# Joining the low three bits of float64 weight words on VectorE: one OR in place of scaling, shift and integer add

## The chip, the cores and the metric

The kernel runs on one core of a Trainium2 chip. The metric is the device time of one execution in microseconds (us), the median of three executions. PE is TensorE (PEld its weight load), DVE VectorE, ACT ScalarE, POOL GpSimd, SP SyncE.

## What is computed

The reference is an attention block followed by a feed-forward block with two weight matrices:

```python
out_d = sm_attn(q_d, k_d, v_d)                  # pooled by 4 along the sequence
out_up = np.repeat(out_d, factor, axis=2)
scores = np.where(mask, scale * q @ k.T, -1e9)  # |i - j| < 4
out_local = softmax(scores) @ v
x = (out_up + out_local) as [4608 tokens, 512]
h = x @ w_in                                    # 512 x 2048
g = np.where(h >= 1, h, np.where(h <= -1, 0.0, (h + 1) ** 2 / 4))
out = g @ w_out                                 # 2048 x 512
```

The two weight matrices are given as float64. The kernel reads them as pairs of 32-bit words and forms the float32 bits itself.

## The kernel before

**Work and stages.** There are 32 attention units (8 batches, 4 pairs of heads), 11 token chunks (one of 512, eight of 384, two of 512) and 16 blocks of the feed-forward width (`f`). In the first stage, to about 144 us, everything stands in a list written out by hand (`ORDER`, L92): units 0 to 7 of the attention, the loading and decoding of all 32 weight blocks (`i0` to `i15` of `w_in`, `o0` to `o15` of `w_out`), and the feed-forward of the first chunk. After it a scheduler weaves the other 24 units between the matmuls of the other chunks (to about 730 us), and the last two chunks are multiplied with fewer products (`strassen`) to the end. Each engine runs its instructions in the order given; semaphores make it wait for others.

**A weight block** comes as `raw` (128 partitions, 512 numbers, two words each). `convert` (L798) decodes it in six pieces, each with a place of its own in `ORDER` (`i4.c1`, `i4.c3` ...):

- piece 1 (L803, ACT): the exponent of the high words is rebased in place;
- piece 3 (L816, DVE): `m` becomes the high words shifted left by three;
- piece 2: the low words, as unsigned numbers, times 2^-29, which rounds to an integer from 0 to 8. On ACT (L812) for 24 blocks, on DVE (L810) for the 8 blocks of `ON_VECTOR` (`o1, o3 ... o15`);
- piece 4 (L819, DVE): integer addition of the two, in place; the trace calls it CUSTOM_DVE_ANT_0, the built program ISA;
- piece 5 (L822, ACT): `m` rounded into the high part `w[:, 0]` of the weight;
- piece 6 (L826, POOL): the rest, `m` minus the high part, into `w[:, 1]`.

PE's products need both parts: each product is high by high, low by high and high by low.

**The tiles** `m`, `u`, `gh` and `gl` rotate through ten buffers of 128x512 (`temp`, L795). `m` is taken from them in piece 3.

**The first chunk's feed-forward** for each `f`: 12 matmuls (L847) into one of two banks, the gate (`u1` DVE L869, `sq` ACT L872, `u2` DVE L875, `gh` ACT L881, `gl` POOL L884), then 12 matmuls (L902).

**The attention units 4 to 7** of this stage share one PSUM tile (two banks, `hi1`): scores (L311, L323) are written to it, DVE takes the maximum (`mxl`, L334) and subtracts it (`sl`, L353), the pooled scores (L377) take the same tile after that, and at the end of the unit DVE's `x` (L541) reads the outputs, upon which the next unit's L311 may write.

Of the kernel before, what the change touches and what calls it, by code (L numbers as in the profile page):

```python
# [11 lines left out]
I32 = mybir.dt.int32  # L12
U32 = mybir.dt.uint32
U8 = mybir.dt.uint8
AF = mybir.ActivationFunctionType
ALU = mybir.AluOpType
# [11 lines left out]
NFC = DFF // P  # L28
# [52 lines left out]


WARM = 10
ON_VECTOR = {("o", f) for f in range(1, NFC, 2)}

PIECES = (3, 4, 2, 1)

# [73 lines left out]
def attention_then_ffn(ctx: ExitStack, tc, qT, kT, vw, vp, vq, band, members, w_in, w_out, out):  # L161
    nc = tc.nc
# [625 lines left out]
    raw, weights = {}, {}  # L788
# [6 lines left out]
    def temp(name, kind=F32):  # L795
        return mpool.tile([P, 512], kind, name=name, tag="t512", bufs=10)

    def convert(name, f, piece):  # L798

        t = raw[name, f]  # L800
        if piece == 1:
            high = t.bitcast(F32)[:, :, 1]
            nc.scalar.activation(high, high, AF.Prelu, scale=2.0**-112, alpha=-(2.0**32))  # L803
        elif piece == 2:
            raw["low", name, f] = t[:, :, 0]
            if (name, f, "m") in raw and (name, f) not in ON_VECTOR:
                raw["low", name, f] = t.rearrange("p n t -> p (n t)")[:, 0:512]
            low = t.bitcast(U32)[:, :, 0]
            if (name, f) in ON_VECTOR:
                nc.vector.tensor_scalar(raw["low", name, f], low, 2.0**-29, None, op0=ALU.mult)  # L810
            else:
                nc.scalar.activation(raw["low", name, f], low, AF.Copy, scale=2.0**-29)  # L812
        elif piece == 3:
            raw[name, f, "m"] = temp("m")
            mi = raw[name, f, "m"].bitcast(I32)
            nc.vector.tensor_scalar(mi, t[:, :, 1], 3, None, op0=ALU.logical_shift_left)  # L816
        elif piece == 4:
            mi = raw[name, f, "m"].bitcast(I32)
            nc.vector.tensor_tensor(mi, mi, raw["low", name, f], op=ALU.add)  # L819
        elif piece == 5:  # L820
            w = wpool.tile([P, 2, 512], F32R, name=f"w_{name}{f}", tag=f"w{name}{f}")
            nc.scalar.copy(w[:, 0], raw[name, f, "m"])  # L822
            weights[name, f] = w
        else:
            w = weights[name, f]
            nc.gpsimd.tensor_tensor(w[:, 1], raw[name, f, "m"], w[:, 0], op=ALU.subtract)  # L826
# [233 lines left out]
    with psum("pair") as two, tc.manual_schedule(), ExitStack() as six:  # L1060
# [7 lines left out]
        for token in ORDER:  # L1068
            token, _, spare = token.partition("+")
            spare = int(spare or 0)  # L1070
            token, _, tag = token.partition("@")
            whose, what = token.split(".")
            kind, f = whose[0], whose[1:]
            if kind in "io":
                if what == "ld":
                    load_weights(kind, int(f))
                else:
                    convert(kind, int(f), int(what[1]))
            elif kind == "f":
                c, f = divmod(int(f), NFC)  # L1080
                if not banks:
                    six.close()
                    single(six, ["h0"], ["o0"], ["o1", "o2"], ["h1"], ["o3"])
                if what[1:].isdigit() and what[0] == "s":
                    keep_up(banks["o0"][:, 0:P], spare)
                    product(c, f, int(what[1]))
                else:
                    gate(c, f, what)
            elif kind == "m":
                second_product(0, int(f), int(what))  # L1090
            elif tag:
                ops[int(whose)][what](own[tag], tag, spare)
            elif spare:
                ops[int(whose)][what](spare)
            else:
                ops[int(whose)][what]()
# [162 lines left out]
```

## Time and profile before

| what | us |
|---|---|
| median of three executions | 897.67 |
| lowest and highest | 896.5, 898.2 |
| the profiled execution, first to last instruction | 900.0 |
| PE busy in it | 885.3 (98%) |
| DVE busy | 563.7 (63%) |
| ACT busy | 467.9 (52%) |
| POOL busy | 375.0 (42%) |

No other time of the profiled execution is given than its span, which stands 2.3 us (0.3%) above the median. Matmuls are pipelined and their ends are modelled, so a busy share of PE tells only where it was idle. In lists of groups the first number behind the bar is the time in which the group ran, the second the mean of one instruction in ns, the third the time the engine sat idle just before it and who ended that. In timelines a bracket holds the idle time before a row. DVE instructions that follow each other without a wait overlap by about 0.07 us, so their durations sum to a little more than their distance.

### The profile page before, as it was taken

The page shows a single profiled execution, that of the slowest core. Times are in us where ns is not written, and L with a number is a line of the kernel's source. Part 1 is how long each engine was busy: PE and PEld are TensorE (multiplying, and loading weights), DVE is VectorE, ACT ScalarE, POOL GpSimd, SP SyncE. Part 2 cuts the span into 40 slices and gives each one's busy share as a digit, 9 for nine tenths or more (in the row PEclk, how much of TensorE's full clock was granted, in tenths as well). Part 3 has the DMA queues.
Part 4 walks back from the last instruction along what each step waited for, and adds up shares of the span by engine and source line. Part 5 has one row for each costly group of instructions (what it writes and reads, how often), then busy time and mean ns, then how long its engine had stood idle before and what let it go on. Part 6 is the DMA issues. An engine that isn't in the chain of part 4 may idle for free.

```text
span 900.0 us, 19773 instructions
## 1 busy us (share of the span) xinstructions
PE 885.3 (98%) x7808; PEld 798.0 (89%) x7808; DVE 563.7 (63%) x1077; ACT 467.9 (52%) x1025; POOL 375.0 (42%) x361
## 2 busy tenths in 40 slices
PE   8999899999999999999999999999999999999998
PEld 6687688899999999999999999989999989999997
DVE  6699995766566477566556656665556546754442
ACT  4798675554544545554454454564454444434333
POOL 3166783444343244444432443344444434433232
PEclk9999999999999999999999999999999999999999
DMA  9369311333233233333332343342233212434341
GB/s 344 120 213 319 126 57 53 97 110 128 90 115 115 91 106 116 122 120 116 113 103 89 101 133 103 105 139 92 91 127 106 83 51 83 122 109 141 105 126 53
DMA packets 67884, 106.47 MB, mean 118 GB/s; under 512 B 5808, under 2 KB 33456, under 8 KB 67792
## 3 DMA queue, kind: packets, MB, share of 16 engines
q1 hardware_dynamic: 67648, 105.17, 35.5%
q8 instruction: 61, 1.00, 0.4%
q14 instruction: 31, 0.25, 0.1%
q10 hardware_dynamic: 144, 0.05, 0.0%
HBM read 71.51 MB, written 17.83 MB: 99 GB/s over the span
## 4 chain that ended last, share of the span: by engine, by line
PE 84%; DVE 7%; ACT 4%; issue 3%; POOL 2%; DMA 0%; SPq 0%; DVEq 0%; ACTq 0%; POOLq 0%
PE ffn_o L902 37%; PE ffn_h L847 28%; PE ffn_h L1015 7%; PE score_ps L643 2%; PE turn_ps L771 1%; PE value_ps L667 1%; DVE m L819 1%; PE local_ps L768 1%; PE value_ps L625 1%; DVE m L816 1%; DVE u L869 1%; DVE u L875 1%; POOL gl L884 1%; ACT u L872 1%; DVE sums L924 1%
## 5 line engine op out<-in xcount | busy, mean ns | idle before, releaser
L884 POOL TENSOR_TENSOR gl<-u,gh 128x384 fp32r<-128x384 f32 (+1 forms) x176 | 197.0, 1120 | 400.4 <-ACT gh L881 320.3
L902 PE MATMUL ffn_o<-w_o,gh 128*128 128x512 f32 x1152 | 347.5, 383 | 0.0
L847 PE MATMUL ffn_h<-xh,w_i 128*128 128x384 f32 (+1 forms) x1184 | 301.2, 336 | 2.5 <-POOL w_i L826 2.1
L902 PEld LDWEIGHTS ffn_o<-w_o,gh 128*128 128x128 f32 x1152 | 212.0, 190 | 25.2 <-issue 0.6
L847 PEld LDWEIGHTS ffn_h<-xh,w_i 128*128 128x128 f32 x1184 | 209.5, 189 | 16.9 <-POOL w_i L826 2.9
L902 PE MATMUL ffn_o<-w_o,gl 128*128 128x512 f32 x576 | 218.9, 380 | 0.4 <-POOL gl L884 0.4
L847 PE MATMUL ffn_h<-xl,w_i 128*128 128x384 f32 (+1 forms) x592 | 197.3, 333 | 0.0
L872 ACT ACTIVATE u<-u 128x384 f32<-128x384 f32 (+1 forms) x176 | 97.4, 553 | 133.5 <-DVE u L869 133.5
L881 ACT CAST gh<-u 128x384 fp32r<-128x384 f32 (+1 forms) x176 | 95.3, 542 | 118.8 <-DVE u L875 117.3
L869 DVE TENSOR_SCALAR u<-m 128x384 f32<-128x384 f32 (+1 forms) x160 | 76.1, 476 | 127.3 <-ACT m L868 126.9
L875 DVE SCALAR_TENSOR_TENSOR u<-m,u 128x384 f32<-128x384 f32 (+1 forms) x160 | 103.2, 645 | 78.0 <-ACT u L872 78.0
L902 PEld LDWEIGHTS ffn_o<-w_o,gl 128*128 128x128 f32 x576 | 109.3, 190 | 16.4 <-POOL gl L884 0.8
L847 PEld LDWEIGHTS ffn_h<-xl,w_i 128*128 128x128 f32 x592 | 111.9, 189 | 2.2
L868 ACT COPY m<-ffn_h 128x384 f32<-128x384 f32 (+1 forms) x132 | 63.8, 484 | 51.1 <-PE ffn_h L847 42.4
L720 ACT ACTIVATE sl<-sl 128x640 f32<-128x640 f32 x24 | 17.7, 739 | 55.1 <-POOL sl L694 55.1
L581 POOL TENSOR_TENSOR xl<-x,xh 128x576 fp32r<-128x576 f32 (+4 forms) x32 | 35.3, 1110 | 16.6 <-ACT xh L580 16.6
L826 POOL TENSOR_TENSOR w_o<-m,w_o 128x512 fp32r<-128x512 f32 x16 | 24.1, 1517 | 31.2 <-ACT w_o L822 31.2
L924 DVE SCALAR_TENSOR_TENSOR sums<-sums 128x128 f32<-128x128 f32 (+1 forms) x72 | 33.0, 459 | 1.6
L694 POOL TENSOR_TENSOR sl<-sl,mxl 128x640 f32<-128x640 f32 x24 | 30.2, 1260 | 2.3 <-DVE mxl L693 1.7
L924 DVE SCALAR_TENSOR_TENSOR words<-sums,words 128x512 fp32r<-128x512 f32 x16 | 17.7, 1109 | 17.7 <-ACT words L928 17.7
L826 POOL TENSOR_TENSOR w_i<-m,w_i 128x512 fp32r<-128x512 f32 x16 | 22.6, 1415 | 11.6 <-ACT w_i L822 11.4
L1041 POOL TENSOR_TENSOR m<-both 128x256 f32<-128x256 f32 x14 | 10.7, 765 | 39.0 <-DVE both L1040 33.8
(179 smaller groups left out, 1183.4 us busy)
## 6 DMA issues: line engine op xcount, KB each, us to landing
xh<-kept SPq DMA_DIRECT2D x56, 256.0 KB, 3.8
v<-vw SPq DMA_DIRECT2D x29, 320.0 KB, 4.0
vq_sb<-vq SPq DMA_DIRECT2D x24, 384.0 KB, 3.0
out<-osb SPq DMA_DIRECT2D x36, 256.0 KB, 2.4
raw_i<-w_in SPq DMA_DIRECT2D x16, 512.0 KB, 8.7
raw_o<-w_out SPq DMA_DIRECT2D x16, 512.0 KB, 8.9
kept<-words SPq DMA_DIRECT2D x32, 256.0 KB, 2.6
k_sb<-kT SPq DMA_DIRECT2D x28, 288.0 KB, 3.3
```

The costliest lines, as they stand in the source:

```text
L581: nc.gpsimd.tensor_tensor(xl[:, p, dst], x[:, part], xh[:, p, dst], op=ALU.subtract)
L826: nc.gpsimd.tensor_tensor(w[:, 1], raw[name, f, "m"], w[:, 0], op=ALU.subtract)
L847: ins = nc.tensor.matmul(htiles[c, f], wi[:, wt, cc * P : (cc + 1) * P], turns(xt[:, cc, ts]), start=(cc == 0 and xt is xh and wt == 0), s ...
L868: utiles["copied"] = nc.scalar.copy(m, h)
L869: nc.vector.tensor_scalar(utiles[c, f], m if c > 0 else h, -1.0, 1.0, op0=ALU.max, op1=ALU.add)
L872: nc.scalar.activation(u, u, AF.Square, scale=0.5)
L875: utiles["last"] = nc.vector.scalar_tensor_tensor(u, utiles["m"] if c > 0 else h, 1.0, u, op0=ALU.max, op1=ALU.min)
L881: nc.scalar.copy(gh, utiles[c, f])
L884: nc.gpsimd.tensor_tensor(gl, utiles.pop((c, f)), gh, op=ALU.subtract)
L902: ins = nc.tensor.matmul(o, gt[:, ts], turns(weights["o", f][:, wt, :]), start=f == 0 and n == 0, stop=f == NFC - 1 and n == 2,)
L924: return nc.vector.scalar_tensor_tensor(out, a, 1.0, b, op0=ALU.mult, op1=op)
L1015: ins = nc.tensor.matmul(ps, left(wt, k), right(xt, k), start=not more and k == 0 and wt == xt, stop=k == 1 and xt == 1, skip_group_check= ...
```

## The change

Pieces 2 and 3 do nothing any more. Piece 4 takes the tile `m` and issues two instructions on DVE: the low words times 2^-29, capped at 7, as integers into `m`; then the high words shifted left by three, OR `m`. The table `ON_VECTOR` goes. `ORDER` stays as it is, so both instructions stand where the addition stood.

```diff
@@ -81,7 +81,6 @@
 WARM = 10
-ON_VECTOR = {("o", f) for f in range(1, NFC, 2)}
@@ -801,22 +800,15 @@
         if piece == 1:
             high = t.bitcast(F32)[:, :, 1]
             nc.scalar.activation(high, high, AF.Prelu, scale=2.0**-112, alpha=-(2.0**32))
-        elif piece == 2:
-            raw["low", name, f] = t[:, :, 0]
-            if (name, f, "m") in raw and (name, f) not in ON_VECTOR:
-                raw["low", name, f] = t.rearrange("p n t -> p (n t)")[:, 0:512]
-            low = t.bitcast(U32)[:, :, 0]
-            if (name, f) in ON_VECTOR:
-                nc.vector.tensor_scalar(raw["low", name, f], low, 2.0**-29, None, op0=ALU.mult)
-            else:
-                nc.scalar.activation(raw["low", name, f], low, AF.Copy, scale=2.0**-29)
-        elif piece == 3:
+        elif piece in (2, 3):
+            return
+        elif piece == 4:
             raw[name, f, "m"] = temp("m")
             mi = raw[name, f, "m"].bitcast(I32)
-            nc.vector.tensor_scalar(mi, t[:, :, 1], 3, None, op0=ALU.logical_shift_left)
-        elif piece == 4:
-            mi = raw[name, f, "m"].bitcast(I32)
-            nc.vector.tensor_tensor(mi, mi, raw["low", name, f], op=ALU.add)
+            nc.vector.tensor_scalar(mi, t.bitcast(U32)[:, :, 0], 2.0**-29, 7.0, op0=ALU.mult, op1=ALU.min)
+            nc.vector.scalar_tensor_tensor(
+                mi, t[:, :, 1], 3, mi, op0=ALU.logical_shift_left, op1=ALU.bitwise_or
+            )
```

In the built program the lines below L84 stand one lower, those below piece 2 eight lower: the scaling is now L808, the join L809, `x` L540, `sl` L352.

DVE's order ahead of the `x` of unit 5, before (names end in buffer numbers; `raw_o10` is the block):

```order
L869 TENSOR_SCALAR u_1249<-ffn_h1_715 128x512
L816 TENSOR_SCALAR m_1264<-raw_o10_1145 128x512
L875 SCALAR_TENSOR_TENSOR u_1249<-ffn_h1_715,u_1249 128x512
L816 TENSOR_SCALAR m_1280<-raw_o9_1109 128x512
L816 TENSOR_SCALAR m_1287<-raw_i12_1213 128x512
L810 TENSOR_SCALAR raw_o9_1109<-raw_o9_1109 128x512
L819 ISA m_1264<-m_1264,raw_o10_1145 128x1024
L819 ISA m_1280<-raw_o9_1109,m_1280 128x1024
L816 TENSOR_SCALAR m_1332<-raw_i11_1167 128x512
L541 TENSOR_TENSOR x_1341<-pl_ps_1311,xd_1339 128x576
```

And with the change:

```order
L861 TENSOR_SCALAR u_1229<-ffn_h1_710 128x512
L867 SCALAR_TENSOR_TENSOR u_1229<-ffn_h1_710,u_1229 128x512
L808 TENSOR_SCALAR m_1274<-raw_o10_1128 128x512
L809 SCALAR_TENSOR_TENSOR m_1274<-raw_o10_1128,m_1274 128x512
L808 TENSOR_SCALAR m_1283<-raw_o9_1092 128x512
L809 SCALAR_TENSOR_TENSOR m_1283<-raw_o9_1092,m_1283 128x512
L540 TENSOR_TENSOR x_1314<-pl_ps_1286,xd_1312 128x576
```

Four weight instructions stand there in place of seven; the shifts of `i12` and `i11` went behind, to their additions.

DVE's order from the maximum of unit 6's scores (`mxl`) to its pooled sums, before:

```order
L816 TENSOR_SCALAR m_1400<-raw_o13_1236 128x512
L334 TENSOR_REDUCE mxl_1405<-sl_ps_1370 128x10
L810 TENSOR_SCALAR raw_o13_1236<-raw_o13_1236 128x512
L353 TENSOR_TENSOR sl_1418<-sl_ps_1370,mxl_1405 128x640
...
L291 TENSOR_REDUCE kd_1478<-k_sb_1428 128x144
L819 ISA m_1332<-m_1332,raw_i11_1167 128x1024
L819 ISA m_1287<-m_1287,raw_i12_1213 128x1024
```

And with the change:

```order
L333 TENSOR_REDUCE mxl_1375<-sl_ps_1342 128x10
L352 TENSOR_TENSOR sl_1387<-sl_ps_1342,mxl_1375 128x640
...
L290 TENSOR_REDUCE kd_1447<-k_sb_1397 128x144
L808 TENSOR_SCALAR m_1453<-raw_i11_1150 128x512
L809 SCALAR_TENSOR_TENSOR m_1453<-raw_i11_1150,m_1453 128x512
L808 TENSOR_SCALAR m_1460<-raw_i12_1187 128x512
L809 SCALAR_TENSOR_TENSOR m_1460<-raw_i12_1187,m_1460 128x512
```

Two instructions went from the path of `sl`, and two came in ahead of the weights `i11` and `i12`.

## Rows read from the trace of the kernel before

**Rows 1.** Stretches: length, busy us (instructions) by engine, PE clock, DMA share, GB/s.

```profile
60.00:80.00 20.00, 18.23 (x136) 14.91 (x133) 19.93 (x28) 18.09 (x34) 16.57 (x11) 1.00 0.82 269
80.00:100.00 20.00, 19.33 (x135) 15.97 (x133) 19.44 (x25) 17.70 (x30) 14.50 (x10) 1.00 0.50 196
...
120.00:140.00 20.00, 19.57 (x181) 16.07 (x180) 16.58 (x25) 12.89 (x22) 17.15 (x12) 1.00 0.21 66
140.00:160.00 20.00, 20.00 (x193) 17.40 (x192) 9.30 (x18) 10.59 (x23) 4.98 (x5) 1.00 0.21 72
```

**Rows 2.** What PE waited for, 0 to 145 us: total, times, longest.

```profile
PE sl_ps L311 <- DVE x L541: 2.3, 1, 2.3
PE ffn_h L847 <- POOL w_i L826: 2.1, 2, 1.8
PE sp_ps L377 <- DVE sl L353: 1.9, 2, 1.2
...
PE ffn_o L902 <- POOL gl L884: 0.4, 1, 0.4
```

**Rows 3.** PE's timeline, 75 to 110 us: start, length, line, shape, count, idle before.

```profile
75.52 0.48 PE L847 MATMUL ffn_h<-xh,w_i 128*128 128x512 f32 x1 [1.77 <-POOL w_i L826]
...
101.88 0.55 PE L311 MATMUL sl_ps<-band_r,ident_r 128*128 128x384 f32 x2 [2.26 <-DVE x L541]
...
103.21 1.22 PE L902 MATMUL ffn_o<-w_o,gh 128*128 128x512 f32 x2
...
109.13 0.71 PE L377 MATMUL sp_ps<-kd,first_qd 64*64 64x144 f32 x12 [0.75 <-DVE sl L353]
```

**Rows 4.** The stretch behind the longest stall, columns as in rows 1.

```profile
102.00:107.00 5.00, 5.00 (x52) 4.06 (x53) 5.00 (x7) 4.02 (x7) 2.09 (x3) 0.66 0.44 124
```

**Rows 5.** DVE's weight instructions L816, 57 to 101.9 us: busy us, count.

```profile
57.00:101.90 44.90, 12.40 (x16) 1.00 0.60 211
```

**Rows 6.** The same for L819.

```profile
57.00:101.90 44.90, 16.11 (x15) 1.00 0.60 211
```

**Rows 7.** The same for L810.

```profile
57.00:101.90 44.90, 2.61 (x3) 1.00 0.60 211
```

**Rows 8.** Three lines by themselves: count, then minimum, median, maximum in ns.

```profile
L810 DVE TENSOR_SCALAR raw_o<-raw_o x8: 418/534/1648, 33.9 to 131.7; 128x512 int32<-128x512 uint32 x8
...
L819 DVE CUSTOM_DVE_ANT_0 m<-m,raw_i x16: 669/693/1815, 31.7 to 133.8; 128x1024 uint16<-128x1024 uint16 x16
...
L826 POOL TENSOR_TENSOR w_i<-m,w_i x16: 1278/1294/1757, 40.3 to 135.9; 128x512 fp32r<-128x512 f32 x16
```

**Rows 9.** DVE by line and shape, whole span: two groups of SCALAR_TENSOR_TENSOR.

```profile
L924 DVE SCALAR_TENSOR_TENSOR words<-sums,words 128x512 fp32r<-128x512 f32 x16 | 17.7, 1109 | 17.7 <-ACT words L928 17.7
...
L875 DVE SCALAR_TENSOR_TENSOR u<-ffn_h,u 128x512 f32<-128x512 f32 x16 | 11.0, 690 | 1.0 <-ACT u L872 0.9
```

**Rows 10.** DVE's timeline ahead of `x` of unit 5 and ahead of `sl` of unit 6.

```profile
93.19 1.61 DVE L816 TENSOR_SCALAR m<-raw_i 128x512 int32<-128x512 int32 x1
94.72 1.56 DVE L810 TENSOR_SCALAR raw_o<-raw_o 128x512 int32<-128x512 uint32 x1
...
99.68 1.48 DVE L816 TENSOR_SCALAR m<-raw_i 128x512 int32<-128x512 int32 x1
101.08 0.74 DVE L541 TENSOR_TENSOR x<-pl_ps,xd 128x576 f32<-128x576 f32 x1
...
104.67 1.33 DVE L816 TENSOR_SCALAR m<-raw_o 128x512 int32<-128x512 int32 x1
...
106.65 1.65 DVE L810 TENSOR_SCALAR raw_o<-raw_o 128x512 int32<-128x512 uint32 x1
```

**Rows 11.** DVE's timeline, two instructions, the second on the first's output.

```profile
80.30 0.25 DVE L411 RECIPROCAL sp_ps<-sp_ps 128x13 f32<-128x13 f32 x1
80.59 0.82 DVE L415 TENSOR_TENSOR sl<-sl,sp_ps 128x640 f32<-128x640 f32 x1
```

**Rows 12.** ACT by line and shape, whole span: the scalings of piece 2.

```profile
L812 ACT ACTIVATE raw_i<-raw_i 128x512 int32<-128x512 uint32 x16 | 12.5, 797 | 0.0
```

## The prediction

> **What bounds the kernel now.** The profiled execution took 900.0 us from first to last instruction, 2.3 above the median of 897.67; the sums below are differences inside that execution, and I take them off the median unchanged. I read the stretches first [rows 1]: from 140 us on PE is busy all the time (20.00 of 20), so the change, whose 32 weight blocks are all decoded before that, can only move the first stage, and what it gains there the rest keeps. Between 60 and 100 us DVE is busy for 19.93 and 19.44 of 20 us, ACT for about 18, and PE is short of 20 by 1.8 and 0.7; between 120 and 140 DVE has 3.4 us to spare. Then PE's waits [rows 2]: 2.3 for DVE's `x`, 2.1 for the low part of an `i` block from POOL, 1.9 in two waits for DVE's `sl`, 0.4 for a `gl`: 6.7 us in all. In PE's timeline [rows 3] the long ones end at 75.52 (1.77 long), 101.88 (2.26) and 109.13 (0.75). After the 2.26 us a pair of matmuls of 512 columns takes 1.22 us; the stretch behind it [rows 4] was granted 0.66 of the clock, so that part of it ran at the lower level (1.2 GHz), and (1 - 0.66) x 5.0 = 1.7 us were lost by that. The wait of 1.77 us had no such fall behind it (the stretch from 60 to 80 has the clock at 1.00). Everything that can be won is thus 6.7 + 1.7 = 8.4 us, nearly 1%. A measurement of this kernel tells about 0.2% (1.8 us) from no change.
>
> **The change part by part.**
>
> *ACT.* 24 scalings of about 0.80 us [rows 12] go, 19 us. ACT is not named in front of PE's long waits; gates and the rounding of weights queue behind the scalings, though. I cost the relief at nothing in the sum, since DVE, full beside it, sets the pace; the bound above is the whole wait of 1.77, whose POOL instruction stands behind a `gl` that needs ACT.
>
> *DVE.* 32 shifts, 32 additions and 8 scalings (72 instructions) become 32 scalings and 32 joins (64). The new scaling is of the same kind as L810: unsigned words with a stride of two, multiplied, to integers; alone that takes 0.42 [rows 8], in the stretch 2.61 / 3 = 0.87 [rows 7]. I take 0.775, the mean of the 16 shifts there (12.40 / 16 [rows 5]), since both read one strided word stream and meet the same neighbours. The cap is a second operation in the same pass and I cost it at nothing. A join of integers isn't in the trace. Below I bound it by a free three-operand instruction, 0.69, above by one beside a busy POOL, 1.11 [rows 9]; I take 1.07, the mean of the 15 additions of the stretch (16.11 / 15 [rows 6]), which also read two tiles. New is a wait: the join needs its own scaling's result, at once. A dependent pair stands 0.04 us apart from end to start [rows 11], where free ones overlap by 0.07, so each pair pays about 0.12 more. A pair is then 0.775 + 1.07 + 0.12 = 1.97 us; its ends are 0.42 + 0.69 + 0.04 = 1.15 and 0.87 + 1.11 + 0.12 = 2.10. The tile `m` is taken at the scaling, later than the shift took it, so a buffer's last reader (a POOL low part, or PE's second product of an earlier `f`) has had longer to finish; queued behind such a wait would be everything on DVE, but the old shifts had the same kind of wait, and I cost it at nothing. The orders of PE, POOL and SP, loads included, stay as they were.
>
> The Trainium skill, "VectorE: DVE Perf Modes", section "The DRAIN you can't avoid", has it that a semaphore between two VectorE instructions costs nothing extra, since the pipe is emptied anyway. By that the 0.12 falls away, the 15 pairs before `x` would be 1.8 us shorter, and the sum below would come to about 5.9 in place of 4.1; the row, in which the waiting instruction starts later than a free one, decides against it.
>
> *The path to `x` of unit 5 (101.08 us), where PE waits longest.* DVE hardly idles from 57 us up to it, so what leaves the queue ahead of it counts in full. It had 16 shifts, 15 additions and 3 scalings there: 12.40 + 16.11 + 2.61 = 31.1 us [rows 5 to 7]. Now it has 15 pairs, 15 x 1.97 = 29.5: 1.6 saved. Counted at the place itself, three instructions go (a shift of 1.61, a scaling of 1.56 and a shift of 1.48 [rows 10], each less the overlap of 0.07): 4.4. The scaling of `o7` (median 0.53 [rows 8]) less its overlap adds 0.46; the waits take 15 x 0.12 = 1.8, and the shift of `o3`, formerly done before 57 us, about 0.4: 2.7 saved. I take 2.3. PE restarts when `x` ends, so its own waits up to there are part of this: it restarts 2.3 us sooner, and the wait that is left is shorter than the 1.77 us that left the clock alone. So the 1.7 us of slow clock go too. Sum so far 4.0.
>
> *Behind it.* `sl` of unit 6 loses a shift of 1.33 and a scaling of 1.65 [rows 10] from its path; PE's 0.75 us wait goes: 0.7. The wait of 0.4 for `gl` goes with the shorter queues: 0.4. Against it, the shifts of `i11` and `i12` are no longer done early: their scalings stand right ahead of their joins, after unit 6's sums, two more instructions of about 0.5 on the way to a low part that PE, some 4 us sooner there, needs at once. I put a new wait of 0.7 for POOL's low part of `i11` there (0 to 1.5). At 42 us the scaling of `i2` comes between maximum and `sl` of unit 4 and delays the wait of PE for that `sl` by 0.46; the low part that PE waits for next moves less, and I put 0.3.
>
> Sum: 2.3 + 1.7 + 0.7 + 0.4 - 0.7 - 0.3 = 4.1 us. 897.7 - 4.1 = **893.6 us**. If nearly all waits of PE and the slow clock go with little new, about 7.4 us: 890.3. With the upper price of a pair (2.10) `x` comes 2.7 - 15 x 0.13 = 0.7 sooner at most; if the clock just holds, the sum is 2.5: 895.2.
>
> **The rivals.**
>
> *DVE gives back behind `x` what is gained before it.* DVE's whole work of weights shrinks by some 2 us, while PE would run 4 us ahead; new waits, for low parts and for `u2` freeing a bank, take the place of the old, or the clock falls at another wait. For it: DVE's 19.9 of 20 us [rows 1]. Against it: the 3.4 us to spare after 120. Gain 0.8 to 3, time 895.7.
>
> *Slower: POOL steps between scaling and join.* Shifts took up to 1.61 and scalings 1.65 where they alternate with POOL [rows 10], against 0.42 alone: each then waits for a POOL instruction of 1.28 or more [rows 8]. The new pair always has a gap of 0.04 us in its middle. If each half waited for half a POOL instruction, a pair would be 0.42 + 0.69 + 0.04 + 1.28 = 2.43. Then `x` comes 15 x 2.43 - 31.1 = 5.4 us later, PE waits that much longer, and only the 0.7 at `sl` is won back: 902.4. It decides from a pair of 31.1 / 15 = 2.07 us on. For it: that row of seven, which met POOL at nearly every step. Against it: in the same 45 us the old ones met it as often and still average 0.775 and 1.07.
>
> The Trainium skill, "SBUF — State Buffer", section "Who interferes with whom", says that a VectorE instruction in a two-port mode, or with two SBUF inputs, and a GpSimd instruction that reads SBUF block each other for the whole instruction. By that each half of a pair can be blocked for a full 1.28, as each of the old instructions could; the rows agree (a minimum of 0.67 and a maximum of 1.82 for the addition [rows 8]), and the chance of this rival stays where the rows put it.
>
> *The change doesn't bring the fast scaling.* With the cap it might run as slowly as a three-operand pass, 0.69 alone in place of 0.42. Then 15 x 0.27 = 4.0 are added before `x`, the 2.3 saved turn into 1.7 lost, the clock falls as before, and the rest evens out: 899.3. Against it: L810 is at 0.42 with the same words and types.
>
> **How the numbers follow.** The forecast has 0.62 (own range 890.3 to 895.2), the first rival 0.22 (894.7 to 896.9), POOL's gap 0.10, the slow scaling 0.06. The range goes from 890.0 to 897.6: it leaves out POOL's gap, most of the slow scaling and little at the lower end. Faster by over 0.2% (below 895.9) is the forecast and nearly half of the first rival, 0.72; the same is the rest of that and half of the slow scaling, 0.15; slower 0.13.
>
> **What would show it.** Right: scalings with a minimum near 0.42 and joins with one near 0.69, pairs near 1.97 between 57 and 100 us; no rows for L810, L812, L816, L819; `x` of unit 5 at about 98.8 and PE's clock at 1.00 behind it; PE's waits for `sl` left only near 43 us; PE full from some 4 us sooner on. Wrong: pairs above 2.07 on average; the clock falling at another place; PE's waits as long as before behind other instructions, above all POOL's low parts after 105 us.

## The result, and the profile after

The changed kernel takes 907.95 us (median of five executions, 907.05 to 909.85); the kernel before, beside it on the same chip, 897.67. The ratio is 1.0099, with a 95% interval of 1.0073 to 1.0125: about 10 us slower (10.3 by the medians, 9 by the ratio), where faster was forecast. The profiled execution's span is 908.0 us. In every run of this study an execution's time is its span plus 1.7 to 1.9 us, so this one is the 909.85, and the profiled execution of the kernel before (span 900.0) took 901.8, 4.1 us above its median and not 2.3.

From 160 us on the two kernels run alike: PE starts matmul 1420 of 7808 at 158.2 us after the change, and both leave about 749 to 750 us behind that point. The stretches of the first stage, with the columns of [rows 1]:

```profile
60.00:80.00 20.00, 18.48 (x170) 14.75 (x169) 19.39 (x24) 11.59 (x20) 11.29 (x8) 1.00 0.65 217
80.00:100.00 20.00, 16.63 (x79) 13.70 (x78) 18.52 (x28) 15.77 (x31) 12.33 (x10) 0.98 0.57 213
100.00:120.00 20.00, 19.50 (x170) 15.68 (x168) 17.76 (x26) 12.83 (x27) 12.60 (x10) 0.93 0.42 141
120.00:140.00 20.00, 20.00 (x174) 16.82 (x175) 19.00 (x23) 9.20 (x17) 14.31 (x10) 1.00 0.23 67
140.00:160.00 20.00, 17.50 (x130) 14.22 (x129) 13.04 (x20) 8.17 (x18) 8.31 (x6) 0.91 0.03 5
```

ACT's busy time (the fourth of the five) has fallen, to 11.59 from 18.09 between 60 and 80 us. DVE's has not: 19.39 and 18.52 against 19.93 and 19.44, and 19.00 between 120 and 140, where there were 3.4 us to spare. PE loses 3.4 us between 80 and 100, and the stage now reaches into the stretch from 140 on. What PE waited for, 0 to 155 us, beside [rows 2]:

```profile
PE ffn_h L839 <- DVE u L867: 4.4, 2, 2.5
PE ffn_h L839 <- POOL w_i L818: 2.3, 4, 0.9
PE sp_ps L376 <- DVE sl L352: 1.7, 1, 1.7
PE tp_ps L468 <- DVE sp L419: 1.2, 1, 1.2
...
PE sl_ps L310 <- DVE x L540: 0.8, 1, 0.8
PE ffn_h L839 <- ACT w_i L814: 0.6, 1, 0.6
```

The wait of 2.3 for `x` of unit 5 is gone, as are those for `sl` near 109 and for `gl`. In their place stand two waits for the gate's `u2`, which frees a bank of `ffn_h`, one for `sp` and one for `x` of unit 4. PE's timeline behind the two waits for `u2`:

```profile
98.64 0.70 PE L839 MATMUL ffn_h<-xh,w_i 128*128 128x512 f32 x2 [1.89 <-DVE u L867]
...
99.41 1.06 PE L839 MATMUL ffn_h<-xh,w_i 128*128 128x512 f32 x2
...
103.02 0.59 PE L839 MATMUL ffn_h<-xh,w_i 128*128 128x512 f32 x2
```

```profile
146.43 0.70 PE L839 MATMUL ffn_h<-xh,w_i 128*128 128x512 f32 x2 [2.50 <-DVE u L867]
...
147.19 1.06 PE L839 MATMUL ffn_h<-xh,w_i 128*128 128x512 f32 x2
```

Behind each, a pair of matmuls of 512 columns takes 1.06 for some 3 us, and then 0.59 again: the clock fell to its lower level (1.2 GHz) behind these two waits (a granted clock of 0.53 from 99.4 to 103.0 us and from 147.2 to 150.8), and no longer behind a wait for `x`. Matched matmul by matmul, each fall costs 1.6 to 1.7 us.

The new instructions by themselves, in the view of one line (count, minimum, median, maximum in ns):

```profile
L808 DVE TENSOR_SCALAR m<-raw_o x16: 416/546/1558, 29.1 to 141.1; 128x512 int32<-128x512 uint32 x16
...
L809 DVE SCALAR_TENSOR_TENSOR m<-raw_o,m x16: 693/862/1758, 29.7 to 142.7; 128x512 int32<-128x512 int32 x16
L809 DVE SCALAR_TENSOR_TENSOR m<-raw_i,m x16: 691/835/1892, 30.8 to 138.0; 128x512 int32<-128x512 int32 x16
```

At the least they cost what the forecast took as the price of one alone, 0.42 and 0.69. Of the 14 joins that meet no POOL instruction only six do (0.69 to 0.73); the other eight take 0.83 to 0.88, and no run shows why. The sum is not what was forecast: the 32 scalings take 24.8 us and the 32 joins 34.7, 59.4 together, as much as the 72 instructions they replaced (22.0 + 30.9 + 6.2 = 59.1, added up over all shifts, additions and scalings). In a second execution of the kernel before (before_again, below) the 72 took only 55.7. DVE's timeline ahead of the first of the two late gates (L861 is `u1` of f7, L867 its `u2`):

```profile
87.88 1.43 DVE L808 TENSOR_SCALAR m<-raw_o 128x512 int32<-128x512 uint32 x1
89.34 1.66 DVE L809 SCALAR_TENSOR_TENSOR m<-raw_o,m 128x512 int32<-128x512 int32 x1
90.92 0.50 DVE L808 TENSOR_SCALAR m<-raw_o 128x512 int32<-128x512 uint32 x1
91.46 0.83 DVE L809 SCALAR_TENSOR_TENSOR m<-raw_o,m 128x512 int32<-128x512 int32 x1
92.20 0.52 DVE L808 TENSOR_SCALAR m<-raw_i 128x512 int32<-128x512 uint32 x1
92.76 0.86 DVE L809 SCALAR_TENSOR_TENSOR m<-raw_i,m 128x512 int32<-128x512 int32 x1
...
96.05 0.67 DVE L861 TENSOR_SCALAR u<-ffn_h 128x512 f32<-128x512 f32 x1
97.89 0.69 DVE L867 SCALAR_TENSOR_TENSOR u<-ffn_h,u 128x512 f32<-128x512 f32 x1 [1.17 <-ACT u L864]
```

```profile
87.62 2.83 POOL L876 TENSOR_TENSOR gl<-u,gh 128x512 fp32r<-128x512 f32 x2
```

The first pair meets POOL (two instructions, 87.62 to 90.45, with the join at 89.34 beginning in the second), and takes 3.1 us from 87.88 to 91.00. The next meets nobody and still needs 1.28 from start to start (90.92 to 92.20). And ACT, which rounds the weights in order, now waits for joins (0 to 150 us):

```profile
ACT w_i L814 <- DVE m L809: 14.0, 11, 2.0
ACT w_o L814 <- DVE m L809: 11.1, 7, 3.2
```

That is 25.1 us of waiting, where ACT waited 4.7 us for additions before; the 20 us between them are about as much as the 19 us of scalings that ACT was spared. The second half of the late gate hangs on that as well: `u2` at 97.89 waited 1.17 for ACT's `sq`, which stood behind such a rounding.

### The profile page after: what moved, and what is told of

Same layout as the page of the kernel before. It is cut to its first block, busy times and chain, and to the rows that moved or that the text cites. A ratio compares the mean times of both kernels' runs of the same rounds, so it can differ in the third digit from the quotient of the medians.

```text
span 908.0 us, 19732 instructions
## 1 busy us (share of the span) xinstructions
PE 889.4 (98%) x7808; PEld 799.7 (88%) x7808; DVE 567.7 (63%) x1069; ACT 453.0 (50%) x1001; POOL 370.7 (41%) x361
## 4 chain that ended last, share of the span: by engine, by line
PE 82%; DVE 10%; ACT 4%; issue 3%; DMA 1%; POOL 0%; SPq 0%; ACTq 0%; DVEq 0%; POOLq 0%
PE ffn_o L894 35%; PE ffn_h L839 28%; PE ffn_h L1007 7%; DVE m L808 2%; PE score_ps L642 2%; DVE m L809 2%; PE turn_ps L770 1%; DVE u L867 1%; PE value_ps L666 1%; PE pl_ps L525 1%; PE local_ps L767 1%; PE value_ps L624 1%; ACT u L864 1%; DVE u L861 1%; DMA pooled<-sp_rest 1%
## 5 line engine op out<-in xcount | busy, mean ns | idle before, releaser
L876 POOL TENSOR_TENSOR gl<-u,gh 128x384 fp32r<-128x384 f32 (+1 forms) x176 | 194.8, 1107 | 397.3 <-ACT gh L873 319.6
L839 PE MATMUL ffn_h<-xh,w_i 128*128 128x384 f32 (+1 forms) x1184 | 304.8, 339 | 7.4 <-DVE u L867 4.4
L864 ACT ACTIVATE u<-u 128x384 f32<-128x384 f32 (+1 forms) x176 | 97.3, 553 | 133.4 <-DVE u L861 133.2
L861 DVE TENSOR_SCALAR u<-m 128x384 f32<-128x384 f32 (+1 forms) x160 | 76.1, 476 | 127.7 <-ACT m L860 127.5
L867 DVE SCALAR_TENSOR_TENSOR u<-m,u 128x384 f32<-128x384 f32 (+1 forms) x160 | 103.1, 644 | 77.8 <-ACT u L864 77.8
L818 POOL TENSOR_TENSOR w_o<-m,w_o 128x512 fp32r<-128x512 f32 x16 | 21.7, 1364 | 37.9 <-DVE m L808 25.2
```

The source lines that it names most:

```text
L839: ins = nc.tensor.matmul(htiles[c, f], wi[:, wt, cc * P : (cc + 1) * P], turns(xt[:, cc, ts]), start=(cc == 0 and xt is xh and wt == 0), s ...
L861: nc.vector.tensor_scalar(utiles[c, f], m if c > 0 else h, -1.0, 1.0, op0=ALU.max, op1=ALU.add)
L864: nc.scalar.activation(u, u, AF.Square, scale=0.5)
L867: utiles["last"] = nc.vector.scalar_tensor_tensor(u, utiles["m"] if c > 0 else h, 1.0, u, op0=ALU.max, op1=ALU.min)
L876: nc.gpsimd.tensor_tensor(gl, utiles.pop((c, f)), gh, op=ALU.subtract)
```

## The experiments

All medians in us, each beside the kernel before on the same chip:

| run | median | before | ratio (95%) |
|---|---|---|---|
| the change | 907.95 | 897.67 | 1.0099 (1.0073 to 1.0125) |
| scale_at_3 | 897.71 | 898.52 | 0.9989 (0.9980 to 0.9998) |
| both_at_3 | 909.61 | 898.52 | 1.0118 (1.0104 to 1.0131) |
| old_shift_at_4 | 912.55 | 898.52 | 1.0147 (1.0132 to 1.0162) |
| tile_at_3 | 907.86 | 898.52 | 1.0093 (1.0079 to 1.0107) |
| pair_free | 900.98 | 898.24 | 1.0041 (1.0026 to 1.0055) |
| late_three | 897.88 | 898.24 | 1.0001 (0.9989 to 1.0014) |
| early_seven | 902.76 | 898.24 | 1.0052 (1.0034 to 1.0070) |
| act_scale | 895.20 | 898.24 | 0.9966 (0.9952 to 0.9980) |
| before_again | 897.92 | 897.70 | 1.0005 (0.9987 to 1.0022) |
| free_at_3 | 901.20 | 897.70 | 1.0047 (1.0028 to 1.0066) |
| scale_at_2 | 899.70 | 897.70 | 1.0022 (1.0012 to 1.0032) |
| act_all | 897.35 | 897.70 | 1.0001 (0.9991 to 1.0012) |
| spacer | 907.70 | 898.36 | 1.0097 (1.0078 to 1.0116) |
| act_early | 895.45 | 898.36 | 0.9964 (0.9953 to 0.9975) |
| act_scale_2nd | 895.60 | 898.36 | 0.9965 (0.9953 to 0.9978) |

### Where the two instructions stand, and whether they are a pair

Four theories were set against each other: "late" (work that DVE did early now lies on the way to ACT's rounding), "POOL between" (a pair back to back is what costs), "tile" (`m` is taken from its buffers later), "join" (the OR is dearer than the addition).

**scale_at_3**: the scaling goes to piece 3, the join stays.

```diff
-        elif piece in (2, 3):
+        elif piece == 2:
             return
-        elif piece == 4:
+        elif piece == 3:
             raw[name, f, "m"] = temp("m")
             mi = raw[name, f, "m"].bitcast(I32)
             nc.vector.tensor_scalar(mi, ..., 2.0**-29, 7.0, op0=ALU.mult, op1=ALU.min)
+        elif piece == 4:
+            mi = raw[name, f, "m"].bitcast(I32)
             nc.vector.scalar_tensor_tensor(
```

> The changed kernel's two instructions, but the scaling (and with it the tile m) at piece 3's place, where the old shift stood; only the join is left at piece 4. Theory 'late' (the first half of the work on a weight block no longer stands where DVE had time for it, and the pair now lies on the way to ACT's rounding, and so to the gates behind it): most of the 10.3 us come back, 896 to 900. Theory 'POOL between' (a pair of instructions back to back is split by POOL, and its price is what costs): also 896 to 900, since the halves no longer follow each other. Theory 'tile' (m is taken later, behind another reader of its buffer): 896 to 900. Theory 'join' (the OR itself is dearer in the stretch than the integer addition): 905 to 908.

Measured 897.71: the whole loss is gone, with the same two instructions per block. "Join" falls. The scalings now take 22.0 us and the joins 29.1, some 51 in place of 59.4.

**both_at_3**: the same, with the join too at piece 3 and nothing at piece 4.

> The changed kernel with the whole pair, scaling and join back to back, at piece 3's place; nothing at piece 4. Theory 'late': 894 to 899, since joins are done well ahead of ACT's rounding. Theory 'POOL between': 905 to 909, as the pair stays a pair. Theory 'tile': 896 to 900. Theory 'join': 905 to 909.

Measured 909.61, worse than the change. "Late" in its first form falls: the joins are all done early, and the time is as bad. The places of loss are others: PE's wait for `u2` of f0 and one for `x` of unit 4, with the clock falling behind each, and two more of 1.5 to 1.8 for `x` of unit 5 and `sl` of unit 6.

```profile
52.74 0.70 PE L839 MATMUL ffn_h<-xh,w_i 128*128 128x512 f32 x2 [2.00 <-DVE u L867]
...
54.35 1.06 PE L839 MATMUL ffn_h<-xh,w_i 128*128 128x512 f32 x2
...
69.78 0.56 PE L310 MATMUL sl_ps<-band_r,ident_r 128*128 128x384 f32 x2 [1.94 <-DVE x L540]
```

**old_shift_at_4**: the kernel before with its own arithmetic, the shift and `m` moved to piece 4.

```diff
         elif piece == 3:
-            raw[name, f, "m"] = temp("m")
-            mi = raw[name, f, "m"].bitcast(I32)
-            nc.vector.tensor_scalar(mi, t[:, :, 1], 3, None, op0=ALU.logical_shift_left)
+            return
         elif piece == 4:
+            raw[name, f, "m"] = temp("m")
             mi = raw[name, f, "m"].bitcast(I32)
+            nc.vector.tensor_scalar(mi, t[:, :, 1], 3, None, op0=ALU.logical_shift_left)
             nc.vector.tensor_tensor(mi, mi, raw["low", name, f], op=ALU.add)
```

> The kernel before with its own arithmetic (scaling at piece 2 on ACT or VectorE, integer addition), only the shift and the tile m moved to piece 4, right ahead of the addition. Theory 'late': 901 to 906, a good half of the loss, since one of the two late instructions is there and the other, the scaling, is not. Theory 'POOL between': 903 to 908, a pair again. Theory 'tile': 905 to 908. Theory 'join': 896 to 900, since the OR is not there.

Measured 912.55, above what any theory gave. The old instructions lose as much as the new ones once they stand together at piece 4, so the loss is not in what the instructions compute.

**tile_at_3**: the changed kernel, with only the line that takes `m` moved to piece 3.

> The changed kernel with the tile m taken from its ten buffers at piece 3, as before, and both instructions left at piece 4. Theory 'late', theory 'POOL between' and theory 'join': 906 to 909, as the changed kernel. Theory 'tile': 896 to 901.

Measured 907.86: "tile" falls.

### The wait inside the pair, or the crowd at one place

What was left was "wait" (the join's wait for its own scaling) and "crowd" (two instructions where one stood, ahead of something on DVE that others need).

**pair_free**: both instructions at piece 4, but the join doesn't need its scaling; it takes a zero in place of the scaled words, so this kernel leaves out the low three bits.

```diff
-            nc.vector.tensor_scalar(mi, t.bitcast(U32)[:, :, 0], 2.0**-29, 7.0, ...)
+            low = t.bitcast(U32)[:, :, 0]
+            nc.vector.tensor_scalar(t[:, :, 0], low, 2.0**-29, 7.0, ...)
             nc.vector.scalar_tensor_tensor(
-                mi, t[:, :, 1], 3, mi, op0=ALU.logical_shift_left, op1=ALU.bitwise_or
+                mi, t[:, :, 1], 3, nothing.broadcast_to([P, 512]), op0=..., op1=ALU.bitwise_or
             )
```

> The changed kernel with both instructions at piece 4, but the join no longer needs its scaling: the scaling writes its result back into the low words, and the join takes an integer zero in their place, so the low three bits of the weights are left out. Same count, same place, no wait inside the pair. Theory 'wait' (the join's wait for its scaling, some 0.15 us each and a gap in which POOL steps in, makes the pair dear): joins by themselves at 0.69 again, the 32 pairs together near the 51 us of the run with the scaling at piece 3 in place of 59, and a time of 896 to 901. Theory 'crowd' (two instructions in one place stand ahead of an instruction of VectorE that others need, a first gate step, a maximum, an output, where one stood before): 903 to 907, a little better than the changed kernel.

Measured 900.98, 2.7 above its kernel before, where the change is 10.3 above: 7.5 us less by the medians, 5.2 by the ratios. The edit takes out the wait inside the pair, but it does two things more: the scaling writes every second word of `raw`, and the join reads one zero per partition in place of a tile. No run has the one without the other. The same stretch of DVE as above, ahead of `u1` of f7 (L864 here):

```profile
87.46 0.53 DVE L811 TENSOR_SCALAR raw_o<-raw_o 128x512 int32<-128x512 uint32 x1
87.87 0.70 DVE L812 SCALAR_TENSOR_TENSOR m<-raw_o,nothing 128x512 int32<-128x512 int32 x1
88.47 0.56 DVE L811 TENSOR_SCALAR raw_i<-raw_i 128x512 int32<-128x512 uint32 x1
...
92.92 0.69 DVE L864 TENSOR_SCALAR u<-ffn_h 128x512 f32<-128x512 f32 x1
```

Here the join begins 0.12 before its scaling ends, as free instructions do, and the pair is 1.01 from start to start.

**free_at_3**: the same without the wait, at piece 3, where the pair had cost as much.

> The kernel with the whole pair at piece 3 (909.6), but without the wait inside the pair: the scaling writes into the low words, the join takes a zero in their place, so the low three bits are left out. Theory 'wait': 898 to 902, as the pair without its wait at piece 4 (901.0). Theory 'crowd': 905 to 909, as two instructions still stand where one stood, ahead of gates and outputs.

Measured 901.20, 3.5 above its kernel before, against 909.61 with the wait, 11.1 above: 7.6 us by the medians, 6.4 by the ratios, at another place, from the same edit. This is the strongest evidence for "wait". The length of a pair, from the start of its first instruction to the end of its second, over all 32 in the trace:

| run | mean us | undisturbed (under 1.6): count, mean | over 2.2 |
|---|---|---|---|
| the change | 1.90 | 19, 1.34 | 11 |
| both_at_3 | 1.92 | 17, 1.32 | 11 |
| old_shift_at_4 | 1.88 | 18, 1.38 | 11 |
| pair_free | 1.56 | 20, 1.19 | 5 |
| free_at_3 | 1.63 | 20, 1.15 | 8 |

An undisturbed pair is 0.15 to 0.17 us longer with the wait (some 5 us in 32), and there are 3 to 6 more pairs over 2.2. Together that is 60.7 - 49.9 = 10.8 us of DVE's time at piece 4. In the undisturbed pairs the whole difference lies between the two instructions: the join begins 0.04 after its scaling's end with the wait and 0.10 before it without, while scaling and join together take 1.30 in both. So there the other two things that the edit does cost or save nothing. For the disturbed pairs they aren't excluded, though joins that read a whole tile took over 1.2 us in only 4 of 32 cases in scale_at_3, against 2 in pair_free, 5 in free_at_3 and 10 in the change.

**late_three**: scale_at_3 with the scaling of `i8`, `i9` and `i10` back at piece 4 (`if (name, f) in (("i", 8), ("i", 9), ("i", 10))`).

> The kernel with the scaling at piece 3, but for three blocks alone (i8, i9, i10, whose joins stand right ahead of the first gate step of f7) the scaling goes back to piece 4. Theory 'crowd': the three scalings, some 0.5 us each and 0.15 more in their joins, put off that gate step by about 2 us; PE waits for the bank that it frees and loses some 1.6 us to the lower clock behind the wait: 3 to 4 us lost, 900.5 to 902. Theory 'wait': three pairs in place of 32, about a tenth of the 10 us: 898 to 899.

Measured 897.88, no loss against the kernel before. "Crowd" as it was stated falls: the scalings do put off `u1` and PE's wait there grows, but from 1.12 to 1.44 and without a fall of the clock:

```profile
94.46 0.70 PE L845 MATMUL ffn_h<-xh,w_i 128*128 128x512 f32 x2 [1.44 <-DVE u L873]
...
95.22 0.59 PE L845 MATMUL ffn_h<-xh,w_i 128*128 128x512 f32 x2
```

**early_seven**: the reverse, the changed kernel with the scaling at piece 3 for seven blocks, those ahead of the two late gates.

> The changed kernel with the scaling at piece 3 for seven blocks alone (o8, i10, i9, i8 ahead of the first gate step of f7; i15, o14, o15 ahead of that of f13, the two places where PE waited longest for a gate and ran slowly behind it); the other 25 blocks stay as pairs at piece 4. Theory 'crowd': the two waits (1.9 and 2.5) and the slow matmuls behind them (1.6 each) go for the most part, 5 to 7 us gained: 901 to 903. Theory 'wait': seven of 32 pairs, 2 us: 905 to 907.

Measured 902.76, 5.8 us better than the change from 7 of 32 blocks (4.5 above its kernel before, in place of 10.3). Here "wait" by count falls: it matters which pairs. Of the two waits for `u2` one is left, 1.2 us, and no fall; the change's other new waits (1.7 for `sl`, 1.2 for `sp`, 0.8 for `x`, 0.6 for a rounded block) are all still there, as are the 25 other pairs:

```profile
PE ffn_h L845 <- DVE u L873: 1.2, 1, 1.2
```

So neither theory holds alone. A pair with the wait is longer; what that costs depends on where pairs gather ahead of an instruction that PE needs.

**scale_at_2**: the scaling at piece 2, two to four DVE instructions ahead of the join as a rule.

> The changed kernel with the scaling (and m) at piece 2's place, as a rule two to four instructions of VectorE ahead of the join; 3 of the 32 joins still follow their scaling directly, where all 32 do in the changed kernel. The scalings are nearly as late as in the changed kernel. Theory 'wait': 897.5 to 899.5. Theory 'crowd': 900 to 904, since the scalings stand in the same stretches, ahead of the same gate steps.

Measured 899.70, 2.0 above its kernel before, between the ranges of the two theories. Nearly as late as in the change, but apart, and four fifths of the loss are gone.

**spacer**: the changed kernel with a short instruction on a tile of its own (128x16) between scaling and join; run twice, and the trace read here is of the second.

```diff
             nc.vector.tensor_scalar(mi, ..., 2.0**-29, 7.0, op0=ALU.mult, op1=ALU.min)
+            nc.vector.tensor_scalar(between[:, 1], between[:, 0], -1.0, None, op0=ALU.mult)
             nc.vector.scalar_tensor_tensor(
```

> The changed kernel with one short instruction of VectorE (128x16, on a tile of its own) between each scaling and its join: order, place and dependency stay, 32 instructions of about 0.1 us are added. Theory 'POOL through the gap' (the pair is dear because POOL gets in while the join waits, so a VectorE that doesn't stop keeps it out): joins of over 1.2 us fall from 10 to 2 to 5, time 899 to 904. Theory 'wait' in the narrow sense (the join's later start by itself, or any two instructions with a dependency): 906 to 910, the joins as before and 3 us of added instructions on top.

> The run 'spacer' a second time, for an undisturbed trace; its time was 907.7, as the changed kernel. If the gap lets POOL in and the short instruction closes it, joins of over 1.2 us are 2 to 5 and the time is lost to the 32 added instructions (32 x 0.17 = 5.4 us, or more where POOL meets them). If the short instruction does not close it, joins of over 1.2 us are 8 to 12, as in the changed kernel, and the joins start 0.03 us behind the short instruction, as they did behind the scaling.

Measured 907.70 (and 906.12 in the second), as the change. DVE's timeline over the stretch shown twice above:

```profile
86.94 1.39 DVE L810 TENSOR_SCALAR m<-raw_o 128x512 int32<-128x512 uint32 x1
88.24 1.27 DVE L811 TENSOR_SCALAR between<-between 128x16 f32<-128x16 f32 x1
89.42 0.68 DVE L812 SCALAR_TENSOR_TENSOR m<-raw_o,m 128x512 int32<-128x512 int32 x1
...
91.32 0.49 DVE L810 TENSOR_SCALAR m<-raw_i 128x512 int32<-128x512 uint32 x1
91.74 0.15 DVE L811 TENSOR_SCALAR between<-between 128x16 f32<-128x16 f32 x1
91.85 0.84 DVE L812 SCALAR_TENSOR_TENSOR m<-raw_i,m 128x512 int32<-128x512 int32 x1
```

Joins of over 1.2 us fell from 10 to 5, but five of the short instructions took 1.25 to 1.40 in their place, and a pair with the instruction between is 1.90 long, exactly as without. Undisturbed, the short instruction disappears in the wait: the join starts 0.53 behind its scaling (91.85 - 91.32), where it was 0.54 to 0.56 without. So the theory that the gap is what lets POOL in, and that closing it keeps POOL out, falls in this form. That fewer pairs are disturbed without the wait is measured; why is not settled.

### The kernel before a second time

**before_again**: no edit.

> The kernel before, unchanged, profiled a second time, since the profiled execution that the prediction was worked out on is 2.3 us above the median of its kernel. Theory 'outlier' (the wait of 2.26 us for the x of unit 5 and the slow matmuls behind it, 4.0 of the 4.1 us forecast, belong to that one execution): a span near 896, no wait above 1.9 us between 60 and 145 us, a clock of 1.00 between 100 and 110. If they belong to the kernel: a span near 898 to 900 with the wait and the fall again.

Its span is 894.0, 6.0 below the execution that the prediction was worked out on. The stretch of [rows 4], where the clock was 0.66:

```profile
102.00:107.00 5.00, 4.70 (x31) 3.70 (x31) 4.71 (x8) 3.54 (x6) 4.78 (x4) 1.00 0.93 295
```

What PE waited for, 0 to 145 us:

```profile
PE ffn_h L847 <- POOL w_i L826: 2.1, 2, 1.7
PE sp_ps L377 <- DVE sl L353: 1.5, 2, 1.2
```

There is no wait for `x`. DVE's timeline ahead of it, the same instructions as in [rows 10]:

```profile
93.09 1.64 DVE L816 TENSOR_SCALAR m<-raw_i 128x512 int32<-128x512 int32 x1
94.66 0.56 DVE L810 TENSOR_SCALAR raw_o<-raw_o 128x512 int32<-128x512 uint32 x1
...
96.39 0.41 DVE L816 TENSOR_SCALAR m<-raw_i 128x512 int32<-128x512 int32 x1
97.81 0.76 DVE L541 TENSOR_TENSOR x<-pl_ps,xd 128x576 f32<-128x576 f32 x1 [1.01 <-ACT xd L537]
```

The scaling takes 0.56 in place of 1.56 and the last shift 0.41 in place of 1.48, and DVE even waits 1.0 us for ACT ahead of `x`. What differs is who waits for whom: in the first execution the two engines alternate, each DVE instruction about as long as the POOL instruction beside it; in this one four DVE instructions pass in a row (94.66 to 96.80) while one low part of POOL takes 3.66 us (94.29 to 97.95). The two executions are near the ends of what this kernel does (895.8 to 902.8 over all its runs here; four in about a hundred lie above 901.8, the time of the first). A time like the first one's is rare; whether the wait of 2.26 and the fall behind it are as rare, two traces don't tell.

### Without the shift alone

**act_scale**: the kernel before with the OR, the scaling left at piece 2.

```diff
-                nc.scalar.activation(raw["low", name, f], low, AF.Copy, scale=2.0**-29)
+                nc.scalar.activation(raw["low", name, f], low, AF.Copy, scale=0.93 * 2.0**-29)
         elif piece == 3:
             raw[name, f, "m"] = temp("m")
-            mi = raw[name, f, "m"].bitcast(I32)
-            nc.vector.tensor_scalar(mi, t[:, :, 1], 3, None, op0=ALU.logical_shift_left)
         elif piece == 4:
             mi = raw[name, f, "m"].bitcast(I32)
-            nc.vector.tensor_tensor(mi, mi, raw["low", name, f], op=ALU.add)
+            nc.vector.scalar_tensor_tensor(
+                mi, t[:, :, 1], 3, raw["low", name, f], op0=ALU.logical_shift_left, op1=ALU.bitwise_or
+            )
```

With the factor 0.93 the scaled word never reaches 8, so ACT needs no cap; the low three bits are rounded a little differently for it.

> The kernel before with the OR alone: the scaling stays at piece 2 (24 blocks on ACT, by 0.93 of 2^-29 so that it needs no cap, 8 on VectorE with the cap), m is still taken at piece 3 and the shift is done by the join at piece 4. VectorE loses 32 shifts (22.0 us) and keeps one instruction at each place. Theory 'crowd' and theory 'wait' alike: no pair, no added latency, so no loss: 893 to 897. If VectorE's work does not bound the stage at all: 897 to 899, the same as before. If ACT's scalings are what bounds: 897 to 899 too, with ACT as full as before.

> The run with ACT's scalings and the OR a second time, beside the other two. If its gain over the kernel before is real: a ratio of 0.995 to 0.998 again. If it was chance: 0.999 to 1.001.

Measured 895.20 and again 895.60, ratios 0.9966 and 0.9965: 3 us faster than the kernel before, with **act_early** the only version that beats it by more than 0.1%. A stretch of its profile:

```profile
80.00:100.00 20.00, 20.00 (x141) 17.22 (x140) 15.45 (x20) 19.50 (x35) 14.47 (x11) 1.00 0.55 214
```

DVE has over 4 us to spare where it was full; ACT is nearly full now. Where the 3 us come from isn't shown. PE's waits between 6 us and the stage's end add up to 5.55 in this trace and to 5.55 in before_again, but these are executions of nearly the same time (896.23, one of this kernel's slowest, and 895.83, the fastest of its eight); in act_scale_2nd's trace (894.15) they add up to 4.62. Its executions lie closer together, 894.2 to 896.5, and the kernel before's at 895.8 and above.

**act_early** (the eight DVE scalings at piece 3's place):

> The run with ACT's scalings and the OR (895.2), with the 8 scalings of VectorE at piece 3's place in place of piece 2's, away from POOL's low parts. If their 1.15 us each (9.2 in all, alone 0.42) still cost time: 893 to 894.5. If not: 894.5 to 896.5.

895.45, the same: the scalings fall from a median of 1.35 us to 0.55, and it is worth nothing.

**act_all** (those eight on ACT too):

> The run with ACT's scalings and the OR (895.2), with the last 8 scalings on ACT too (by 0.93 of 2^-29, no cap): VectorE has 32 joins and nothing else of the weight words, 9.2 us less than there; ACT has 8 scalings of about 0.8 us more. If VectorE still bounds the stage: 893 to 895. If ACT is by now as near to the bound as VectorE: 895 to 897.

897.35, 2 us worse than act_scale, above both ranges. DVE falls to 11.05 us in that stretch and nothing is won; eight scalings more on ACT cost time:

```profile
80.00:100.00 20.00, 19.88 (x139) 16.79 (x137) 11.05 (x17) 19.77 (x33) 13.62 (x10) 1.00 0.52 201
```

## Why the prediction was wrong

**The base.** "[T]he sums below are differences inside that execution, and I take them off the median unchanged" is the first step that failed. Two terms, `x` of unit 5 sooner (2.3) and the clock's 1.7, made 4.0 of the 4.1 us. Both did go in the changed kernel, as foretold, but before_again shows that an execution of the old kernel can be without them, and scale_at_3, which also has neither, measures within 0.1% of the old median. They could be won only from an execution that stands 4.1 above the median. Without them the sum would have been 0.1, no change; so this step explains the missing gain and not the loss.

**The places.** The prediction followed what the move adds at two places, a wait of 0.7 for a low part behind 105 us and 0.3 for `sl` near 43. Both are there in about that size: 0.5 for a low part at 119.95, and 1.7 for `sl` in place of 1.2. It left the rest at nothing: "PE restarts when `x` ends, so its own waits up to there are part of this". That is the second step that failed, and the one that turned the sign. Against before_again, PE reaches the end of the stage 12.7 us later: its waits add up to 12.5 in place of 5.55, 7.0 more, and the two falls of the clock take 3.3; 0.9 of the rest was there by 8 us already, when neither kernel has decoded a block, and the last 1.5 no row accounts for. None of the five larger new waits (`sp` 1.2 and `x` 0.8 of unit 4, a rounded block 0.6, `u2` of f7 and f13) was looked for, since they hardly showed in the trace of before (0.3 us for `u2` of f7, the others not at all). With the first of the two instructions early again, in scale_at_3, only 1.1 us for `u2` of f7 is left of them. `x` of unit 5 came at 105.58 in place of 101.08:

```profile
105.58 0.76 DVE L540 TENSOR_TENSOR x<-pl_ps,xd 128x576 f32<-128x576 f32 x1 [0.73 <-ACT xd L536]
```

The last thing it waited for was ACT's `xd`, and that had waited 3.5 us for PE, late itself by then; DVE's queue alone would have let `x` begin near 104.8.

**The price of a pair.** 1.97 was forecast; the 15 pairs from 57 us to `x` of unit 5 are 2.01 long, and 1.90 is the mean of all 32. So the size was right, and that DVE's instructions for the weights would shrink was not: 59.4 us against 59.1, or 55.7 in the second execution. (The prediction's count "at the place itself" takes only two of the three old scalings out. The one of `o5`, 0.46, is missing: 3.1 us, not 2.7. Nothing hangs on it.) The third step that failed is the wait, "about 0.12 more" for each pair. By itself it is that (0.15), but pairs with the wait are disturbed more often, and with both counted the 32 pairs of the change are 10.8 us longer than those of pair_free. The Trainium skill, "VectorE: DVE Perf Modes", section "The DRAIN you can't avoid", has it that a semaphore between two VectorE instructions costs nothing extra, and also that a next instruction which is not held starts earlier. These runs bear out the second and not the first: an undisturbed pair takes 1.34 with the wait and 1.19 without it, where the join starts 0.10 before its scaling's end.

**The rivals.** "POOL steps between scaling and join" came nearest, in its sign and in its rows: ten joins took 1.65 to 1.89. But its turning point, a pair of 2.07 ahead of `x` of unit 5, was just missed (2.01), its price of 902.4 was too low, and the loss didn't arise at that `x`. "DVE gives back" had named the mechanism, `u2` freeing a bank and the clock falling at another wait, but as a smaller gain (895.7), not as a loss, 12 us below what was measured. The slow scaling didn't occur (0.42).

**What held.** ACT's relief at nothing: act_scale keeps ACT's scalings and is among the fastest, while the change frees ACT and makes it wait 25 us for joins. (More work on ACT is not free: act_all's eight scalings cost 2 us.) `m`'s later place at nothing: tile_at_3. A fall of the clock at 1.7 us: right in size, behind other waits. That a wait shorter than 1.77 leaves the clock alone did not hold everywhere: in old_shift_at_4 it fell behind one of 1.76.

**What stays open.** The 7.5 and 7.6 us that pair_free and free_at_3 win back are shown at two places, but not why a pair with the wait meets POOL more often; the spacer excludes only that filling the gap is enough. Nor is it shown that they are the wait's alone, since both runs also change where the scaling writes and what the join reads. Some 3 us between pair_free (901.0) and scale_at_3 (897.7) belong to the place, without a run that splits them further.

## What to carry to other kernels

Two instructions in place of two is no equal trade if one of the old ones was done early: look at what each moved instruction stands in front of in its new place, on its own engine and on those that wait in order for its result, and not only at the waits that the old trace shows. Don't put a result and its only reader back to back on VectorE where there is room between; the same two instructions apart cost nothing here (scale_at_3) or 2 us (scale_at_2) in place of 10. And when the profiled execution stands above the median, profile a second one before a wait in it is sold as a gain.

## What the runs showed of the hardware

- Integer shift and OR in one pass over two tiles of 128x512 takes 0.69 us at the least, as much as a three-operand pass in float [rows 9], and the unsigned scaling with its cap 0.42, as without it. Eight of 14 such joins beside no POOL instruction took 0.83 to 0.88.
- In the change a join starts 0.03 to 0.04 us behind the scaling it needs in 30 of 32 pairs (0.10 in two); a free one in pair_free starts 0.07 to 0.16 before the scaling's end. A short independent instruction (0.15) fits into the wait without making the pair longer (1.90 both ways).
- An instruction of 128x16, 0.15 us alone, took 1.25 to 1.40 in five of 32 cases, all beside a POOL instruction: a short VectorE instruction can be held up about as long as a long one.
- The clock fell behind waits of 1.89, 2.00, 2.26 and 2.50 us and not behind 1.12 and 1.44, but in between the length of a wait doesn't tell it: in old_shift_at_4 it fell behind one of 1.76 and not behind one of 1.92, and in tile_at_3 not behind one of 1.88 at the place where it fell behind 1.89 in the change.
- One kernel's executions spread over 7 us (895.8 to 902.8, about a hundred of them). Two that were traced differ in how POOL's and VectorE's instructions met. Other versions spread less: act_scale over 2.4 us in 21 executions, scale_at_3 over 0.7 in 11.
